# A four-layer forward and backward pass on one core: gradient operands stored by column group, the last attention products on the common ring, dz products three tiles late

## The chip, the cores and the metric

The kernel runs on one core of one Trainium2 chip. A core has TensorE (PE in the profile: matmuls and transposes; PEld is its weight loads), VectorE (DVE), ScalarE (ACT), GpSimd (POOL) and SyncE (SP), and 16 DMA engines that all DMA queues share. Matmul results land in PSUM and are copied out by VectorE or ScalarE; everything else lives in SBUF (128 partitions) or in DRAM. The metric is the device time of one execution in microseconds (us), as a median over runs.

## The reference

Four residual layers on x [2048, 512], A, B, A, B, sharing weights between the two A and between the two B, and then the gradients of x and of all five weight matrices for a given grad_out, in bf16:

```python
def _A_ref(x, wqkv, wo):                       # linear attention, 32 heads of 16
    q, k, v = heads(x @ wqkv)
    phi = lambda t: jnp.where(t > 0, t + 1, jnp.exp(t)) + 1e-6
    pq, pk = phi(q), phi(k)
    kv = jnp.einsum("bhsd,bhse->bhde", pk, v)
    z = jnp.einsum("bhsd->bhd", pk)
    num = jnp.einsum("bhqd,bhde->bhqe", pq, kv)
    den = jnp.einsum("bhqd,bhd->bhq", pq, z)[..., None] + 1e-6
    return merge_heads(num / den) @ wo
def _B_ref(x, w_gate, w_up, w_down):           # F = 1376
    return (_sigmoid(x @ w_gate) * (x @ w_up)) @ w_down
x = x + _A_ref(_layernorm(x), A_wqkv, A_wo)
x = x + _B_ref(_layernorm(x), B_w_gate, B_w_up, B_w_down)
x = x + _A_ref(_layernorm(x), A_wqkv, A_wo)
x = x + _B_ref(_layernorm(x), B_w_gate, B_w_up, B_w_down)
out = x;  gradients = vjp of this with grad_out
```

A weight gradient is a product over all 2048 rows: for instance the gradient of w_up is (normalised x)^T times the gradient of the product x @ w_up, [512, 2048] x [2048, 1376], summed over both B layers.

## The kernel before, in words

The 2048 rows are 16 tiles of 128 (NST = 16); 512 columns are four chunks of 128 (NDC), 1376 columns eleven, the last of 96 (NFC). Layers are numbered 0 (A), 1 (B), 2 (A), 3 (B).

**Forward.** Per A layer kq_fwd and then ab_fwd, which interleaves the attention output of one tile with the gated layer of the next. ab_fwd keeps what the backward pass needs in DRAM: h (the normalised input), ssd, and the gated product hh (stored at L705 into part 0 of `hdd`, a DRAM tile [2048, 3, 1376], L108).

**Backward, pass 1** goes through the row tiles and carries the gradient of x. b_bwd_p1 (gated layers) loads ssd per tile, makes dd (gradients of the up and gate products, two halves of 1376) and stores it at L839 into parts 1 and 2 of `hdd`. a_bwd_p1 (attention) has two loops. The first, per tile: a POOL cast of the gradient (L994), transposes through PSUM (L287), the products dp (L1002), an ACT copy of dp (L1005), on VectorE a product (L1007) and a sum per head, cneg (L1009), a POOL copy of cneg to bf16 (L1012), four small matmuls dz (L988) that add up in one PSUM tile, a POOL product t_t (L1017), and three VectorE operations (L1020, L1024, L1025) that make dq, stored two tiles at a time (L1028) into the left half of `dqk`, [2048, 1024] (L101). The dz matmuls of a tile are written down after the next tile's dp. Then G = g^T pqn, 64 matmuls (L1035), with the last tile's dz ahead of its second quarter. The second loop makes dk, stores it into the right half of `dqk` (L1133) and loads dq again (dq_ld, L1090).

**Backward, pass 2** makes the weight gradients. The columns are cut into groups of 256 (the last one 96); a "set" is a tile [128, 16, 256] that holds one such group for all rows, loaded by p2_set (L879–882) out of the row-major DRAM tile, so 2048 pieces of 512 B. p2_cols_group (L889–912) multiplies it with h_all: 64 matmuls of 128x256 (L903); the first layer of a pair leaves its result as a partial in DRAM, the second (final) loads that partial into dw_stg (L894), adds it on VectorE (L908) and writes the output (L912). b_bwd_p2 (L915–942) does w_down (L933, evacuation in dw_evac, L858–869), w_up and w_gate; a_bwd_p2 (L945–951) the q and k columns of wqkv, in four sets. Their resources R are a ring of three set buffers, two staging buffers and two PSUM buffers, all loads on SP's DMA queue.

**The last part.** The order of the calls is written out (L223–237): b_bwd_p1(3), a_bwd_p1(2), b_bwd_p2(3), b_bwd_p1(1), a_bwd_p2(2), a_bwd_p1(0), b_bwd_p2(1), a_small_grads, a_bwd_p2(0). The last two use resources RT of their own: pool t_big, three more set buffers (t_sets), four PSUM buffers (t_psum), and loads on ACT's DMA queue (L875, L881, L894). a_small_grads (L1168–1190) makes the gradient of wo and of the v columns of wqkv: 8 and 32 small matmuls, eight ACT copies into two fin_o buffers, eight outputs of 128 KB.

The code is written in a tile framework: its scheduler fixes one static order for each engine from the order of the calls, priorities and its own cost model, and uses pass 2's matmuls to fill gaps of pass 1. Semaphores between engines and DMAs follow from the tiles. On one queue, instructions issue in order, each waiting for its own inputs and free buffers.

Of the kernel before, what the change touches and what calls it, by code (L numbers as in the profile page):

```python
# [16 lines left out]
S = 2048  # L17
# [11 lines left out]
EPS = 1e-6  # L29
NB = 4  # L30


# [18 lines left out]
def kernel(  # L51
# [42 lines left out]
    for l in range(4):  # L94
        d = {}
        d["h"] = dram.tile([S, D], BF16, name=f"sv_h{l}")
        d["gbf"] = dram.tile([S, D], BF16, name=f"sv_gbf{l}")
        if l % 2 == 0:
            for nm in ("hT", "pqn", "phq", "pk"):
                d[nm] = dram.tile([S, D], BF16, name=f"sv_{nm}{l}")  # L100
            d["dqk"] = dram.tile([S, 2 * D], BF16, name=f"sv_dqk{l}")  # L101
            d["X"] = dram.tile([D, D], BF16, name=f"sv_X{l}")
            for nm, w in SMALL:
                d[nm] = dram.tile([D, w], BF16, name=f"sv_{nm}{l}")
            d["MT"] = dram.tile([D, D], BF16, name=f"sv_MT{l}")
        else:
            d["ssd"] = dram.tile([S, 2, F], BF16, name=f"sv_ssd{l}")
            d["hdd"] = dram.tile([S, 3, F], BF16, name=f"sv_hdd{l}")  # L108
        k.sv[l] = d
# [75 lines left out]
    if True:  # L185
# [26 lines left out]
        def mk_out1_cb(o1stg):  # L212
            o1cur = {}

            def out1_cb(st):
# [3 lines left out]
                if st % 2 == 1:  # L219
# [9 lines left out]
        b_bwd_p2(k, R, 1, True, list(range(NFC)))  # L229
        RT = P2Res(k,  # L230
                   big=bctx.enter_context(tc.tile_pool(name="t_big", bufs=1)),
                   sets=bctx.enter_context(tc.tile_pool(name="t_sets", bufs=3)),
                   stage=R.stage,
                   psum=bctx.enter_context(tc.tile_pool(name="t_psum", bufs=4, space=PSUM)),
                   set_w=2 * P, dma=[nc.scalar], pfx="ta")
        a_small_grads(k, RT.big, R.stage, RT.psum)
        a_bwd_p2(k, RT, 0, True)


# [339 lines left out]
def ab_fwd(k, A, ln, nxt=None, out_cb=None, extra=(), x_src=None):  # L579
# [3 lines left out]
    with ExitStack() as ctx:  # L583
# [85 lines left out]
        for st in range(NST):  # L669
# [34 lines left out]
            nc.sync.dma_start(out=sv["ssd"][rows(st), :, :], in_=ssd_t[:])  # L704
            nc.sync.dma_start(out=sv["hdd"][rows(st), 0, :], in_=hh_t[:])  # L705
            prev = T
# [64 lines left out]
def b_bwd_p1(k, l):  # L771
# [4 lines left out]
    with ExitStack() as ctx:  # L776
# [41 lines left out]
        for st in range(NST):  # L818
            g_bf, gT = gp.prep(st)
            ssd = ld.tile([P, 2, F], BF16, name="ssd_ld")  # L820
            nc.sync.dma_start(out=ssd[:], in_=sv["ssd"][rows(st), :, :])
            T = dict(st=st, h=hld.get(st), g=g_bf,
                     dd=wide.tile([P, 2, F], BF16, name="dd_t"),
                     ddT=wide.tile([P, 2, NFC, P], BF16, name="ddT"))
            dd = T["dd"]
            for fs in range(3):
                c0, w = FSL[fs]
                dhh_ps = ps_dhh.tile([P, 512], F32, name="dhh_ps")
                for jc in range(NDC):
                    nc.tensor.matmul(dhh_ps[:, 0:w], lhsT=gT[:, jc, :], rhs=k.wdT[:, jc, c0:c0 + w],  # L830
                                     start=(jc == 0), stop=(jc == NDC - 1))
                nc.vector.tensor_tensor(dd[:, 0, c0:c0 + w], dhh_ps[:, 0:w], ssd[:, 0, c0:c0 + w], ALU.mult)  # L832
                nc.vector.tensor_tensor(dd[:, 1, c0:c0 + w], dhh_ps[:, 0:w], ssd[:, 1, c0:c0 + w], ALU.mult)  # L833
                if fs >= 1:
                    transposes(T, fs - 1)
            if prev is not None:
                finish(prev)
            transposes(T, 2)
            nc.sync.dma_start(out=sv["hdd"][rows(st), 1:3, :], in_=dd[:])  # L839
            prev = T  # L840
# [3 lines left out]
class P2Res:  # L844

    def __init__(self, k, big, sets, stage, psum, set_w=P, dma=None, pfx="p2"):
        self.k, self.big, self.sets, self.stage, self.psum, self.set_w = k, big, sets, stage, psum, set_w
        self.pfx = pfx
        self.dma = dma or [k.nc.sync]
        self.i = 0  # L850
# [20 lines left out]

def p2_load_all(k, R, src, name):
    t = R.big.tile([P, NST, D], BF16, name=name)
    for b in range(NST // NB):
# [3 lines left out]

def p2_set(k, R, src2d, c0, w):  # L879
    t = R.sets.tile([P, NST, R.set_w], BF16, name="p2_set")  # L880
    R.eng().dma_start(out=t[:, :, 0:w], in_=src2d[:, c0:c0 + w].rearrange("(n p) f -> p n f", p=P))  # L881
    return t


# [30 lines left out]
def b_bwd_p2(k, R, l, final, fcs, h_all=None, g_all=None):  # L915
# [6 lines left out]
    for g0 in range(0, len(fcs), nper):  # L922
# [3 lines left out]
        w = sum(widths)  # L926
        st_t = p2_set(k, R, sv["hdd"][:, 0, :], c0, w)
        for j, fc in enumerate(grp):
# [10 lines left out]
        for i, nm in ((1, "wu"), (2, "wg")):  # L939
            st_t = p2_set(k, R, sv["hdd"][:, i, :], c0, w)  # L940
            p2_cols_group(k, R, h_all, st_t, w, k.dwp[nm], k.outs[nm], c0, final)
# [3 lines left out]
def a_bwd_p2(k, R, l, final):  # L945
    sv = k.sv[l]
    h_all = p2_load_all(k, R, sv["h"], R.pfx + "_a1")
    nper = R.set_w // P
    for j0 in range(0, 2 * NDC, nper):
        st_t = p2_set(k, R, sv["dqk"], j0 * P, nper * P)  # L950
        p2_cols_group(k, R, h_all, st_t, nper * P, k.dwp["wqkv"], k.outs["wqkv"], j0 * P, final)


def a_bwd_p1(k, R, l, mk_out_cb=None):
# [6 lines left out]
    with ExitStack() as ctx:  # L961
# [8 lines left out]
        with tc.tile_pool(name=f"ab_all{l}", bufs=1) as allp, \  # L970
# [21 lines left out]
            for st in range(NST):  # L992
# [8 lines left out]
                for jc in range(NDC):  # L1001
                    nc.tensor.matmul(dp_ps[:], lhsT=gT[:, jc, :], rhs=k.MT[:, jc, :],  # L1002
                                     start=(jc == 0), stop=(jc == NDC - 1))
                dp = work.tile([P, D], BF16, name="dp")
                nc.scalar.copy(dp[:], dp_ps[:])  # L1005
# [4 lines left out]
                                        negate=True)  # L1010
                cneg_bf = small.tile([P, H], BF16, name="cneg_bf")
                nc.gpsimd.tensor_copy(cneg_bf[:], cneg[:])  # L1012
                if dzq:
                    accum_dz(*dzq.pop())
                dzq.append((st, cneg_bf))
                t_t = work.tile([P, D], BF16, name="t_t")
                nc.gpsimd.tensor_tensor(t_t[:].rearrange("p (h e) -> p h e", h=H),  # L1017
# [8 lines left out]
                if st % NB2 == NB2 - 1:  # L1026
                    b = st // NB2
                    nc.sync.dma_start(out=sv["dqk"][batch_rows(b, NB2), 0:D].rearrange("(n p) d -> p n d", p=P),  # L1028
                                      in_=phld.cur[:])
            for jc in range(NDC):  # L1030
                if jc == 1:
                    accum_dz(*dzq.pop())
                ps = ps_mm.tile([P, D], F32, name="dp_ps")
# [49 lines left out]
        with tc.tile_pool(name=f"ab_stg2{l}", bufs=2) as stg, \  # L1083
# [5 lines left out]
            pkld = BatchLoader(k, stg, sv["pk"], "pk_ld", nb=NB2)  # L1089
            dqld = BatchLoader(k, stg, sv["dqk"], "dq_ld", nb=NB2)  # L1090
            hTld = BatchLoader(k, stg, sv["hT"], "hT_ld", nb=NB2)
# [16 lines left out]
            for st in range(NST):  # L1108
                pk_st = pkld.get(st)
                dq_st = dqld.get(st)  # L1110
                hT_st = hTld.get(st)
# [19 lines left out]
                if st % NB2 == NB2 - 1:  # L1131
                    b = st // NB2
                    nc.sync.dma_start(  # L1133
                        out=sv["dqk"][batch_rows(b, NB2), D:2 * D].rearrange("(n p) d -> p n d", p=P),
                        in_=dkst[:])
                if prev is not None:
# [9 lines left out]


SMALL = (("G", D), ("XT", D), ("kvbd", P), ("dkvbd", P))

# [71 lines left out]
```

## Time and profile before

| what | value |
|---|---|
| median of 3 runs | 1381.03 us (1379.69 to 1385.11) |
| the profiled execution's own time | 1379.42 us |
| its span in the profile | 1377.7 us |
| TensorE busy | 1234.0 us, 90% |
| mean granted TensorE clock | 0.972 |
| packets under 512 B, under 2 KB, in all | 28688, 240528, 259066 |
| DMA queue q1 (SP): MB, share of 16 engines | 247.30, 56.0% |
| DMA queue q10 (ACT): MB, share of 16 engines | 7.34, 1.9% |
| sv_hdd<-dd_t, 32 stores of 688 KB, issue to landing | 3.7 us |
| sv_hdd<-hh_t, 32 stores of 344 KB | 2.3 us |
| p_set<-sv_hdd, 30 wide sets of 1024 KB | 7.5 us |

The stages on the profile's time axis (us): forward up to 510; b_bwd_p1(3) 520 to 674; a_bwd_p1(2) first loop to 738, second loop to 825; b_bwd_p2(3) to 905; b_bwd_p1(1) to 1055; a_bwd_p1(0) first loop 1086 to 1144, second loop 1150 to 1228; b_bwd_p2(1) to 1337; a_small_grads to 1344; the last q and k sets to 1373.7; end 1377.7.

How to read it: an engine's busy time counts only its instructions' own time. A timeline line has start, duration, engine, line, operation, output and inputs, shape and count; in brackets is the idle time before it and what ended that. A windows line has, for each engine, busy time and number of instructions, then the granted TensorE clock as a share of full speed, the mean busy share of the 16 DMA engines (it can pass 1.00, since packets overlap) and the rate.

### The profile page before, as it was taken

Reading aid. Unit: us, or ns where it says so; the run is one execution under the profiler, and the core shown is the slowest. Engines: PE = TensorE matmul, PEld = TensorE weight load, DVE = VectorE, ACT = ScalarE, POOL = GpSimd, SP = SyncE. Lnnn points to the kernel's source line nnn. Section 1 sums busy time; section 2 is a strip of 40 time slices with the busy share of each in tenths; the row PEclk is TensorE's granted clock in tenths of the full one; section 3 lists DMA queues with packets and bytes.
Section 4 is the critical chain, followed back from the end, with each engine's and each line's share of the span. In section 5 each row is a group of like instructions: output and inputs, shape, how many; then the busy total and the mean of one; then the engine's idle time right before and its main releaser. Section 6 shows DMA issues by size and latency. Waiting matters only on the chain. (4 is left out here: it accounts for less than half of the span.)

```text
span 1377.7 us, 22244 instructions
## 1 busy us (share of the span) xinstructions
PE 1234.0 (90%) x8628; PEld 719.4 (52%) x8628; DVE 700.1 (51%) x1344; ACT 568.6 (41%) x1060; POOL 313.9 (23%) x534
## 2 busy tenths in 40 slices
PE   5958888896899978999889999999999989996998
PEld 2424444442455544555455557765555645564777
DVE  5577545456865435556485650035564385641211
ACT  6435666662566753444333441134443323520000
POOL 5046444402644430000351000001101440110000
PEclk9979999998899998999999999999999999998999
DMA  9413433332334459654765649796555946559963
GB/s 317 163 56 138 153 133 145 139 138 92 116 151 174 186 199 323 223 188 163 220 184 170 193 138 323 170 274 228 188 184 189 291 131 203 183 148 312 253 161 94
DMA packets 259066, 256.06 MB, mean 186 GB/s; under 512 B 28688, under 2 KB 240528, under 8 KB 258960
## 3 DMA queue, kind: packets, MB, share of 16 engines
q1 hardware_dynamic: 246480, 247.30, 56.0%
q10 hardware_dynamic: 12480, 7.34, 1.9%
q8 instruction: 67, 1.10, 0.3%
q14 instruction: 39, 0.32, 0.1%
HBM read 135.69 MB, written 118.92 MB: 185 GB/s over the span
## 5 line engine op out<-in xcount | busy, mean ns | idle before, releaser
L903 PE MATMUL p_ps<-p_set,p_a 128*128 128x256 bf16 (+1 forms) x1792 | 193.7, 266 | 11.1 <-DVE dw_stg L908 7.9
L903 PEld LDWEIGHTS <-p_a 128*128 128x128 bf16 x1792 | 160.9, 99 | 33.4 <-issue 8.1
L799 ACT COPY ddT<-T_ps 128x1024 bf16<-128x1024 bf16 (+1 forms) x96 | 83.0, 868 | 105.0 <-PE T_ps L797 104.9
L692 POOL TENSOR_TENSOR ssd_t<-hh_t,oms 128x512 bf16<-128x512 bf16 (+1 forms) x96 | 102.6, 1070 | 100.3 <-ACT oms L690 47.6
L720 DVE SCALAR_TENSOR_TENSOR junk<-t_sb,h_ld 128x512 bf16<-128x512 f32 x64 | 45.8, 716 | 142.6 <-ACT t_sb L718 142.6
L811 PEld LDWEIGHTS <-ddT 128*128 128x128 bf16 (+1 forms) x704 | 66.0, 97 | 69.3 <-issue 10.5
L718 ACT ACTIVATE t_sb<-dh_ps,rstd_all 128x512 f32<-128x512 f32 x64 | 44.0, 687 | 134.9 <-issue 60.8
L811 PE MATMUL dh_ps<-wuT,ddT 128*128 128x512 bf16 (+1 forms) x352 | 95.7, 379 | 4.2 <-ACT t_sb L718 0.9
L722 POOL TENSOR_SCALAR ab<-c 128x2 f32<-128x2 f32 x64 | 12.3, 193 | 373.9 <-DVE junk L720 373.9
L683 PE MATMUL g_ps<-wg,hT 128*128 128x512 bf16 (+1 forms) x384 | 96.6, 366 | 0.0
L686 PE MATMUL u_ps<-wu,hT 128*128 128x512 bf16 (+1 forms) x384 | 94.6, 363 | 0.0
L832 DVE TENSOR_TENSOR dd_t<-dhh_ps,ssd_ld 128x512 bf16<-128x512 f32 (+1 forms) x96 | 60.5, 630 | 57.2 <-issue 49.8
L830 PE MATMUL dhh_ps<-wdT,gT 128*128 128x512 bf16 (+1 forms) x384 | 87.0, 362 | 2.5 <-ACT gT L296 2.5
L691 DVE TENSOR_TENSOR hh_t<-u_ps,ssd_t 128x512 bf16<-128x512 f32 (+1 forms) x96 | 60.7, 633 | 55.9 <-PE u_ps L686 29.5
L933 PE MATMUL p_ps<-p_a,p_set 128*128 128x512 bf16 (+1 forms) x352 | 83.6, 379 | 1.4 <-DMA p_set<-sv_hdd 1.4
L652 PE MATMUL y_ps<-wd,hhT 128*128 128x512 bf16 (+1 forms) x352 | 81.6, 380 | 0.2 <-DVE x L654 0.2
L811 PE MATMUL dh_ps<-wgT,ddT 128*128 128x512 bf16 (+1 forms) x352 | 81.3, 379 | 0.0
L797 PEld LDWEIGHTS <-dd_t 128*128 128x128 bf16 (+1 forms) x704 | 50.2, 100 | 40.7 <-DVE dd_t L832 18.6
L797 PE MATMUL T_ps<-ident,dd_t 128*128 128x128 bf16 (+1 forms) x704 | 66.0, 219 | 3.6 <-DVE dd_t L832 3.3
L908 DVE TENSOR_TENSOR dw_stg<-p_ps,dw_stg 128x512 bf16<-128x512 f32 (+1 forms) x32 | 20.6, 648 | 87.8 <-PE p_ps L903 64.5
L688 ACT ACTIVATE ssd_t<-g_ps 128x512 bf16<-128x512 f32 (+1 forms) x96 | 53.1, 553 | 27.3 <-PE g_ps L683 26.8
L833 DVE TENSOR_TENSOR dd_t<-dhh_ps,ssd_ld 128x512 bf16<-128x512 f32 (+1 forms) x96 | 60.1, 626 | 0.0
(203 smaller groups left out, 2226.6 us busy)
## 6 DMA issues: line engine op xcount, KB each, us to landing
p_set<-sv_hdd SPq DMA_DIRECT2D x30, 1024.0 KB, 7.5
sv_ssd<-ssd_t SPq DMA_DIRECT2D x32, 688.0 KB, 3.1
ssd_ld<-sv_ssd SPq DMA_DIRECT2D x32, 688.0 KB, 5.4
sv_hdd<-dd_t SPq DMA_DIRECT2D x32, 688.0 KB, 3.7
sv_hdd<-hh_t SPq DMA_DIRECT2D x32, 344.0 KB, 2.3
h_ld<-sv_h SPq DMA_DIRECT2D x32, 256.0 KB, 3.6
p_a<-sv_h SPq DMA_DIRECT2D x12, 512.0 KB, 6.3
sv_h<-h_all SPq DMA_DIRECT2D x8, 512.0 KB, 3.3
```

What stands on the lines that cost most here:

```text
L652: nc.tensor.matmul(y_ps[:], lhsT=T["hhT"][0:r, fc, :], rhs=k.wd[0:r, fc, :], start=(fc == 0), stop=(fc == NFC - 1))
L683: nc.tensor.matmul(g_ps[:, 0:w], lhsT=hT[:, kc, :], rhs=k.wg[:, kc, c0:c0 + w], start=(kc == 0), stop=(kc == NDC - 1))
L686: nc.tensor.matmul(u_ps[:, 0:w], lhsT=hT[:, kc, :], rhs=k.wu[:, kc, c0:c0 + w], start=(kc == 0), stop=(kc == NDC - 1))
L691: nc.vector.tensor_tensor(hh_t[:, c0:c0 + w], u_ps[:, 0:w], ssd_t[:, 0, c0:c0 + w], ALU.mult)
L692: nc.gpsimd.tensor_tensor(ssd_t[:, 1, c0:c0 + w], hh_t[:, c0:c0 + w], oms[:, 0:w], ALU.mult)
L797: nc.tensor.transpose(tps[0:r, a, i, :], dd[:, a, fc * P:fc * P + r], k.ident[:])
L799: nc.scalar.copy(ddT[:, :, fcs[0]:fcs[0] + nfull, :], tps[:, :, 0:nfull, :])
L811: nc.tensor.matmul(dh_ps[:], lhsT=T["ddT"][0:r, a, fc, :], rhs=wT[0:r, fc, :], start=(i == 0), stop=(i == n_mm - 1))
L830: nc.tensor.matmul(dhh_ps[:, 0:w], lhsT=gT[:, jc, :], rhs=k.wdT[:, jc, c0:c0 + w], start=(jc == 0), stop=(jc == NDC - 1))
L832: nc.vector.tensor_tensor(dd[:, 0, c0:c0 + w], dhh_ps[:, 0:w], ssd[:, 0, c0:c0 + w], ALU.mult)
L903: nc.tensor.matmul(psv[:, icl, :], lhsT=lhs_all[:, st, ic * P:(ic + 1) * P], rhs=set_t[:, st, 0:W], start=(st == 0), stop=(st == NST - 1))
L933: nc.tensor.matmul(ps[0:r, :], lhsT=st_t[:, st, j * P:j * P + r], rhs=g_all[:, st, :], start=(st == 0), stop=(st == NST - 1))
```

## The change

Three things change.

1. `hdd` becomes [3, 5, 128, 16, 256] (part, column group, partition, tile, column) with the last 96 columns in a DRAM tile of their own, `hdl` [3, 128, 16, 96]; `dqk` becomes [4, 128, 16, 256]. A wide set is one contiguous megabyte, 8 KB for each partition. The store of hh becomes two DMAs, that of dd three, each store of dq and dk two, and each load of dq two: 144 DMAs more in all. In SBUF nothing changes its place.
2. The resources RT go. The last attention sets use R like all others (three ring buffers, two PSUM buffers, SP's queue), with h_all in a pool of its own; a_small_grads is called after them, on R's PSUM buffers.
3. In a_bwd_p1's first loop dp has three buffers, the bf16 copy of cneg is on ACT with five buffers, and the dz matmuls of a tile are written down three tiles later (DZLAG = 3), what is left of them ahead of the second quarter of G.

```diff
+GW = 256
+NG = F // GW
...
-            d["dqk"] = dram.tile([S, 2 * D], BF16, name=f"sv_dqk{l}")
+            d["dqk"] = dram.tile([2 * D // GW, P, NST, GW], BF16, name=f"sv_dqk{l}")
-            d["hdd"] = dram.tile([S, 3, F], BF16, name=f"sv_hdd{l}")
+            d["hdd"] = dram.tile([3, NG, P, NST, GW], BF16, name=f"sv_hdd{l}")
+            d["hdl"] = dram.tile([3, P, NST, F - NG * GW], BF16, name=f"sv_hdl{l}")
...
-        RT = P2Res(k,
-                   big=bctx.enter_context(tc.tile_pool(name="t_big", bufs=1)),
-                   sets=bctx.enter_context(tc.tile_pool(name="t_sets", bufs=3)),
-                   stage=R.stage,
-                   psum=bctx.enter_context(tc.tile_pool(name="t_psum", bufs=4, space=PSUM)),
-                   set_w=2 * P, dma=[nc.scalar], pfx="ta")
-        a_small_grads(k, RT.big, R.stage, RT.psum)
-        a_bwd_p2(k, RT, 0, True)
+        tail = bctx.enter_context(tc.tile_pool(name="t_big", bufs=1))
+        R.big_h = tail
+        a_bwd_p2(k, R, 0, True)
+        a_small_grads(k, tail, R.stage, R.psum)
...
-            nc.sync.dma_start(out=sv["hdd"][rows(st), 0, :], in_=hh_t[:])
+            nc.sync.dma_start(out=sv["hdd"][0, :, :, st, :].rearrange("g p w -> p g w"),
+                              in_=hh_t[:, 0:NG * GW].rearrange("p (g w) -> p g w", g=NG))
+            nc.sync.dma_start(out=sv["hdl"][0, :, st, :], in_=hh_t[:, NG * GW:F])
...
-            nc.sync.dma_start(out=sv["hdd"][rows(st), 1:3, :], in_=dd[:])
+            for a in range(2):
+                nc.sync.dma_start(out=sv["hdd"][1 + a, :, :, st, :].rearrange("g p w -> p g w"),
+                                  in_=dd[:, a, 0:NG * GW].rearrange("p (g w) -> p g w", g=NG))
+            nc.sync.dma_start(out=sv["hdl"][1:3, :, st, :].rearrange("a p w -> p a w"), in_=dd[:, :, NG * GW:F])
...
+        self.big_h = None
...
-def p2_load_all(k, R, src, name):
-    t = R.big.tile([P, NST, D], BF16, name=name)
+def p2_load_all(k, R, src, name, pool=None):
+    t = (pool or R.big).tile([P, NST, D], BF16, name=name)
-def p2_set(k, R, src2d, c0, w):
+def p2_set(k, R, src):
-    R.eng().dma_start(out=t[:, :, 0:w], in_=src2d[:, c0:c0 + w].rearrange("(n p) f -> p n f", p=P))
+    R.eng().dma_start(out=t[:, :, 0:src.shape[-1]], in_=src)
+
+
+def hdd_group(sv, i, g):
+    return sv["hdd"][i, g, :, :, :] if g < NG else sv["hdl"][i, :, :, :]
...
-        st_t = p2_set(k, R, sv["hdd"][:, 0, :], c0, w)
+        st_t = p2_set(k, R, hdd_group(sv, 0, c0 // GW))
...
-            st_t = p2_set(k, R, sv["hdd"][:, i, :], c0, w)
+            st_t = p2_set(k, R, hdd_group(sv, i, c0 // GW))
-    h_all = p2_load_all(k, R, sv["h"], R.pfx + "_a1")
+    h_all = p2_load_all(k, R, sv["h"], R.pfx + "_a1" if R.big_h is None else "t_a1", R.big_h)
-        st_t = p2_set(k, R, sv["dqk"], j0 * P, nper * P)
+        st_t = p2_set(k, R, sv["dqk"][j0 * P // GW, :, :, :])
+
+
+def dqk_store(k, sv, half, b, nb, src):
+    n = D // GW
+    for g in range(n):
+        k.nc.sync.dma_start(out=sv["dqk"][half * n + g, :, b * nb:(b + 1) * nb, :],
+                            in_=src[:, :, g * GW:(g + 1) * GW])
...
-                dp = work.tile([P, D], BF16, name="dp")
+                dp = work.tile([P, D], BF16, name="dp", bufs=3)
-                cneg_bf = small.tile([P, H], BF16, name="cneg_bf")
-                nc.gpsimd.tensor_copy(cneg_bf[:], cneg[:])
-                if dzq:
-                    accum_dz(*dzq.pop())
+                cneg_bf = small.tile([P, H], BF16, name="cneg_bf", bufs=DZLAG + 2)
+                nc.scalar.copy(cneg_bf[:], cneg[:])
+                if len(dzq) > DZLAG:
+                    accum_dz(*dzq.pop(0))
...
-                    nc.sync.dma_start(out=sv["dqk"][batch_rows(b, NB2), 0:D].rearrange("(n p) d -> p n d", p=P),
-                                      in_=phld.cur[:])
+                    dqk_store(k, sv, 0, b, NB2, phld.cur[:])
-                if jc == 1:
-                    accum_dz(*dzq.pop())
+                while jc == 1 and dzq:
+                    accum_dz(*dzq.pop(0))
...
-            dqld = BatchLoader(k, stg, sv["dqk"], "dq_ld", nb=NB2)
...
-                dq_st = dqld.get(st)
+                if st % NB2 == 0:
+                    dq_cur = stg.tile([P, NB2, D], BF16, name="dq_ld")
+                    for g in range(D // GW):
+                        nc.sync.dma_start(out=dq_cur[:, :, g * GW:(g + 1) * GW],
+                                          in_=sv["dqk"][g, :, st:st + NB2, :])
+                dq_st = dq_cur[:, st % NB2, :]
...
-                    nc.sync.dma_start(
-                        out=sv["dqk"][batch_rows(b, NB2), D:2 * D].rearrange("(n p) d -> p n d", p=P),
-                        in_=dkst[:])
+                    dqk_store(k, sv, 1, b, NB2, dkst[:])
...
+DZLAG = 3
```

## The prediction, made before the changed kernel ran

> **What bounds the kernel now.** I read the page's busy shares first, then its 40 slices, then the windows of the stretches that the change touches, then the timeline there.
>
> The page's parts 1 and 2:
>
> ```profile
> PE 1234.0 (90%) x8628; PEld 719.4 (52%) x8628; DVE 700.1 (51%) x1344; ACT 568.6 (41%) x1060; POOL 313.9 (23%) x534
> ...
> PE   5958888896899978999889999999999989996998
> ...
> DMA  9413433332334459654765649796555946559963
> ```
>
> TensorE is the bound: 90% of 1377.7 us. A change can only give back its idle time or its slow-clock time. The thin place late in the run is slice 37 (1240 to 1274 us): PE 6, DMA 9. Windows of 25 us there, then the other stretches that the change touches (columns: engine busy time, granted clock, DMA share):
>
> ```profile
> core 0: us, PE busy (x) PEld busy (x) DVE busy (x) ACT busy (x) POOL busy (x), PEclk, DMA share, GB/s
> 1225.00:1250.00 25.00, 18.23 (x135) 12.83 (x134) 5.40 (x9) 0.59 (x1) 0.62 (x1) 0.90 1.02 285
> 1250.00:1275.00 25.00, 20.31 (x130) 13.66 (x129) 2.77 (x4) 0.00 (x0) 0.00 (x0) 0.90 1.17 301
> ...
> 1300.00:1325.00 25.00, 25.00 (x201) 19.35 (x199) 4.98 (x8) 0.00 (x0) 0.00 (x0) 1.00 0.80 187
> ...
> 575.00:660.00 85.00, 83.65 (x565) 43.89 (x564) 51.50 (x95) 36.15 (x63) 1.74 (x9) 1.00 0.48 163
> 674.00:738.00 64.00, 52.39 (x377) 30.45 (x377) 44.11 (x85) 21.36 (x38) 34.28 (x49) 0.95 0.59 171
> 1086.00:1144.00 58.00, 48.84 (x335) 25.21 (x335) 43.21 (x88) 18.31 (x34) 23.00 (x32) 1.00 0.52 159
> ```
>
> From 1225 to 1275 us all DMA engines are full and TensorE idles 11.5 of 50 us at a clock of 0.90; once the rush is over (1300) it is full at clock 1.00. In the steady b_bwd_p1 loop (575) the DMA is half free. In the two attention loops (674, 1086) TensorE is 82 to 84% busy. The timeline names the rush. DMAs of the ACT queue and a sum on VectorE:
>
> ```profile
> 1230.18 0.39 ACTq L881 DMA_DIRECT2D p_set<-sv_dqk  x1
> 1231.08 9.92 ACTq L875 DMA_DIRECT2D ta_a<-sv_h  x4
> 1248.56 1.29 DVE L908 TENSOR_TENSOR dw_stg<-p_ps,dw_stg 128x512 bf16<-128x512 f32 x2 [12.27 <-DMA dw_stg<-dwp_wu]
> ```
>
> and TensorE, with idle time before each group in brackets:
>
> ```profile
> 1249.30 9.92 PE L903 MATMUL p_ps<-p_set,p_a 128*128 128x256 bf16 x64 [6.75 <-DVE dw_stg L908]
> 1260.64 7.08 PE L933 MATMUL p_ps<-p_a,p_set 128*128 128x512 bf16 x32 [1.42 <-DMA p_set<-sv_hdd]
> 1270.07 3.65 PE L903 MATMUL p_ps<-p_set,p_a 128*128 128x256 bf16 x32 [2.35 <-DVE dw_stg L868]
> 1274.64 3.65 PE L903 MATMUL p_ps<-p_set,p_a 128*128 128x256 bf16 x32 [0.91 <-DVE dw_stg L868]
> 1279.41 7.15 PE L903 MATMUL p_ps<-p_set,p_a 128*128 128x256 bf16 x64 [1.12 <-DVE dw_stg L908]
> 1337.05 1.89 PE L1178 MATMUL p_ps<-G_ld,kvbd_ld 128*128 128x512 bf16 x8
> 1341.66 1.10 PE L1186 MATMUL p_ps<-dkvbd_ld,XT_ld 128*128 128x128 bf16 x16 [1.80 <-ACT fin_o L1180]
> 1344.10 29.59 PE L903 MATMUL p_ps<-p_set,ta_a 128*128 128x256 bf16 x256 [1.33 <-ACT fin_o L1189]
> ```
>
> The ACT queue brings ta_a and three sets (5 MB) needed only from 1344 on, right beside the sets and the 256 KB dw_stg partials that SP brings for now. VectorE waits 12.27 us for one partial, so no PSUM buffer comes free and TensorE waits 6.75 us.
>
> **The last product stretch (ring).** From 1228.65 (first L933 group) to 1373.70 (last L903) lie 145.05 us. Full rate, by undisturbed groups: a column group is 6.91 (L933, 32 matmuls) + 13.97 (L903, 128), four of them 83.52; the last narrow one 3.45 + 5.45 = 8.90; the four q/k sets are 2 x 13.97 = 27.94. Sum 120.36, surplus 24.69. It is made of the five bracketed stalls in 1249–1279, 6.75 + 1.42 + 2.35 + 0.91 + 1.12 = 12.55; of the slot of the small gradients, 1337.05 to 1344.10 = 7.05; of slow clock, 9.92 − 7.15 = 2.77 and 29.59 − 27.94 = 1.65; 0.67 is in small gaps. In the changed program these 5 MB stand in SP's queue behind the sets that come before them, three ring buffers ahead at most, so the rush has no cause. SP is also the queue of the ta_a, G, XT, kvbd and dkvbd loads now, and these stand between the set loads; and with two PSUM buffers instead of four the last sets have the spacing of all earlier ones (7 us per 64 matmuls against 0.65 us of evacuation each half), which at 1300–1325 gave no idle time. What can be late next is the first q set: it reuses a buffer of the narrow wd5/wu5/wg5 sets, and a lone 1 MB load takes 6.1 us, while the two narrow sets left then cover 5.45: 0.65 late. ta_a's 2 MB (5 us at 400 GB/s) may still run beside it. I put 1.5 us on both (0 to 4). −24.7 + 1.5 = **−23.2**.
>
> **The end.** Now 4.00 us lie between the last matmul (1373.70) and the end. The small gradients come last in the changed program: 8 + 32 matmuls, eight ACT copies, eight 128 KB outputs through two fin_o buffers. Their pace is a row of this trace: first copy 1338.13, last copy ends 1348.16, 10.03 us, each pair waiting for an earlier output. 0.5 us from the last L903 to the first result (half of 1337.05–1338.13) + 10.0 + 1.8 for the last output's landing + 1.0 to the end = 13.3, so **+9.3**. It has no cover: nothing follows. Bounds: +7 (outputs faster, since the DMA is otherwise empty) and +11.
>
> **The attention loops (dz).** The changed program's order on each engine is known: the first dz group stands at the same place on TensorE, since the scheduler already kept two to three tiles between a dz and its tile. So its 2.69 us stall (the wait is for pqn_all's load, 8.5 us on VectorE) stays. What changes: after the last dz 40 matmuls of G (L1035) are left instead of 48 in the first loop, 35 instead of 40 in the second; these no longer stand behind the late tail: 8 x 0.216 = 1.7 and 5 x 0.216 = 1.1. The cneg_bf copy leaves POOL, where it took 0.27 us (median) and up to 0.67 ahead of t_t; the ACT copy of that size starts earlier: −0.5 each loop. VectorE waits for t_t on POOL 4.2 and 5.1 us in the two loops, of which I take 1.5 off each (0 to all). In the second loop 26 fewer filler matmuls (L903, L912) stand before G's end, they run later at 0.109 each: +2.8. Loop 1: −1.7 − 0.5 − 1.5 = −3.7; loop 2: −1.1 − 0.5 − 1.5 + 2.8 = −0.3. **−4.0.** What is queued behind the new wait: ACT now waits for cneg (VectorE's L1009) ahead of the next gT and dp copies, which TensorE's next tile needs; ACT is 33% busy there, and the third dp buffer lets ACT empty dp_ps one tile further ahead of VectorE. If that wait bites in a third of 32 tiles with the 0.6 us of a copy, it is +6, so the loops lie between −9 and +2.
>
> **The layout.** Sets: 2048 pieces of 512 B become 128 stretches of 8 KB. A lone set load took 6.1 us (172 GB/s for 1 MB, issue to landing); stretches with pieces over 1 KB ran at 350 to 410 GB/s against 285 to 301 in the rush. I give each of the 38 wide sets 0.5 us less of DMA time, worth nothing to TensorE where it does not wait. Stores pay: dd (704 KB) was two long pieces per row, about 1.75 us of all engines at 400 GB/s; now it is 1280 pieces of 512 B and 256 of 192 B. At the 285–295 GB/s of the 512 B output rows it is 2.4, and 0.5 for the narrow part: 2.9, **+1.2 a step**; hh +0.55. Cover: a b_bwd_p1 step lasts 9.25 us with the DMA busy 0.52 of it (4.8), so 4.4 us are free; ab_fwd has 0.35 of 10.7 us. TensorE pays nothing in the steady steps. In the first 55 us of the first backward loop the share is 0.86 already, five steps x 1.2 = 6 us at the most; I take **+1** (0 to 6). SP issues 144 more DMAs at 0.36–0.5 us, some 60 us of an engine whose instructions nobody waits for except the ssd_ld behind the dd store (0.8 us later, two tiles ahead of use).
>
> The Trainium skill, page "DMA: Bandwidth & Descriptors", section "Rules for kernel authors", speaks against splitting stores: it asks for few large transfers, and says that one under 64 KB is mostly overhead. By its 2 us of fixed cost a DMA (section "Anatomy of one DMA", stated there for the GpSimd path), my estimate is that 144 more would cost 288 us if they stood on the path; the trace has no instruction of TensorE waiting for a store of sv_hdd, so I keep zero. Section "Latency and other measured facts" of the same page says that row pitches at large powers of two (512 KiB and up) lose DMA rate; the new pitch of a partition is 8 KB, which it does not list and no run here shows yet.
>
> **Sum.** −24.7 + 1.5 + 9.3 − 4.0 + 1.0 = −16.9 on the profiled execution's 1379.42 us (span 1377.7): 1362.5. The median of the three runs is 1381.03, 1.6 higher, so I say **1364**. The best ends of all terms (−24.7, 0, +7, −9, 0 = −26.7) give 1354, the worst (−24.7, +4, +11, +2, +6 = −1.7) 1379.
>
> **Rivals.**
> *The change of dz does not do what it says.* For it: the built order keeps the first dz at the same place. Then the loops give 0 (and the second costs its 2.8): 1368 to 1371, inside the main case.
> *The rush is not only the ACT queue's.* SP now has the same 5 MB in its own queue within the same 145 us; against it, at 1300–1325 a share of 0.80 left TensorE full. If 10 of the 12.55 us of stalls come back, or move to the q sets at 1330: 1374, and 1378 with the slow clock's 4.4 too. It is a ring of three whose next load waits for a matmul to release it.
> *Slower: small pieces at a pitch of 8 KB.* All 128 partitions of a store write 512 B (and 192 B) at the same offset of successive 8 KB blocks; the rows of before (5.5 KB, contiguous) do not show that. It decides from the point at which the dd store's 1.75 us grows past the free time, 1.75 + 4.4 = 6.2 us, below 114 GB/s. At 100 GB/s it takes 7.05, a step lasts 4.8 − 1.75 + 7.05 = 10.1 instead of 9.25, and 32 steps cost 0.87 x 32 = +28: 1392 as a median, and 1410 at 92 GB/s. Against it: outputs of 512 B at a pitch of 3 KB run at 285 or more.
>
> **How the numbers follow.** Main case 1358–1371: 0.58. Both loops at their better ends and no tail stalls, 1350–1358: 0.08. The rush stays in part, 1371–1380: 0.16. About as before, 1380–1388 (stalls and end at their worst together): 0.05. Small pieces, 1388–1410: 0.13. The range 1354 to 1380 leaves out about half of the 0.08, the 0.05 and the 0.13: a little over 0.2. Half a per cent, 6.9 us, is about what a measurement can tell: faster means below 1374.1, slower above 1387.9. Faster: 0.58 + 0.08 + 0.06 of the rush case = 0.72; within: 0.10 + 0.05 = 0.15; slower 0.13.
>
> **What would show it.** Right: no L875 or L881 on the ACT queue; TensorE idle under 4 us between the last attention part and the last L903, clock near 1.00; eight fin_o copies about 10 us long at the very end; b_bwd_p1 steps of 9.25 us with DMA share near 0.65. Wrong: TensorE or VectorE waiting for ssd_ld, h_ld or sets inside b_bwd_p1, a dd store that lands after more than 7 us, waits for p_set<-sv_dqk at the first q set, ACT idle on cneg with TensorE idle on gT.

## The result, and the profile after

The changed kernel takes 1361.98 us (median of 4 runs, 1359.01 to 1365.61) against 1381.01; the ratio is 0.9858 (1.4% less), 95% interval 0.9826 to 0.9891. A second set gave 1362.19 and a ratio of 0.9874 (0.9845 to 0.9902). The forecast was 1364. The profiled execution took 1363.26 us with a span of 1361.4.

Parts 1 and 2 of the page after:

```profile
PE 1225.3 (90%) x8628; PEld 717.1 (53%) x8628; DVE 706.3 (52%) x1344; ACT 573.9 (42%) x1092; POOL 304.4 (22%) x502
...
PE   5957888896799997999979999999999979999987
...
DMA  9413443432244559766654739678665855659873
...
DMA packets 266235, 256.08 MB, mean 188 GB/s; under 512 B 43280, under 2 KB 251024, under 8 KB 261264
```

The dent of PE 6 late in the run is gone; what is thin now is the last slice but one and the last. Windows of the kernel after (columns as in those of before):

```profile
1220.00:1245.00 25.00, 25.00 (x197) 19.07 (x195) 5.37 (x8) 0.00 (x0) 0.00 (x0) 1.00 1.01 324
1245.00:1270.00 25.00, 25.00 (x181) 17.51 (x180) 5.00 (x8) 0.00 (x0) 0.00 (x0) 1.00 1.01 328
1270.00:1295.00 25.00, 25.00 (x190) 18.40 (x188) 4.84 (x7) 0.00 (x0) 0.00 (x0) 1.00 0.73 235
1295.00:1320.00 25.00, 21.53 (x258) 18.51 (x257) 4.79 (x9) 0.00 (x0) 0.00 (x0) 0.98 0.79 186
...
575.00:660.00 85.00, 83.67 (x569) 44.19 (x568) 51.49 (x95) 36.75 (x64) 1.73 (x9) 1.00 0.56 163
674.00:738.00 64.00, 52.07 (x409) 31.39 (x410) 47.70 (x89) 24.20 (x54) 28.44 (x32) 1.00 0.50 160
```

The DMA engines are as full as before (1.01), at a higher rate, but TensorE no longer waits and keeps its clock. One stall is left, at the first q set, and then there is the end:

```profile
1312.82 0.82 DVE L917 TENSOR_TENSOR dw_stg<-p_ps,dw_stg 128x192 bf16<-128x192 f32 x2 [1.57 <-DMA dw_stg<-dwp_wu]
1313.67 0.38 SPq L921 DMA_DIRECT2D out_dram<-dw_stg  x1
1314.14 0.46 SPq L903 DMA_DIRECT2D dw_stg<-dwp_wg  x1
...
1319.17 0.62 DVE L917 TENSOR_TENSOR dw_stg<-p_ps,dw_stg 128x192 bf16<-128x192 f32 x2 [5.53 <-DMA dw_stg<-dwp_wg]
1319.58 29.58 PE L912 MATMUL p_ps<-p_set,t_a 128*128 128x256 bf16 x256 [3.47 <-DVE dw_stg L917]
...
1352.73 1.07 ACT L1198 CAST fin_o<-p_ps 128x512 bf16<-128x512 f32 x2 [1.58 <-DMA out_dram<-fin_o]
...
1355.17 1.07 ACT L1207 CAST fin_o<-p_ps 128x512 bf16<-128x512 f32 x2 [1.37 <-DMA out_dram<-fin_o]
...
1357.59 1.07 ACT L1207 CAST fin_o<-p_ps 128x512 bf16<-128x512 f32 x2 [1.35 <-DMA out_dram<-fin_o]
```

The stall is hardly the q set's: TensorE's last narrow product ends at 1316.10, and the set's first load, issued at 1310.56, lands at 1316.55. VectorE waits 5.53 us for the last narrow partial (dwp_wg), whose load was issued only at 1314.14, right behind an output that waits for VectorE.

Where the time went, by landmarks on TensorE in the two profiles (us). Lines named in the text are those of the kernel before; a fence has those of its own kernel. "First loop" and "second loop" are, as in the prediction, the dp and dz loops of a_bwd_p1(2) and of a_bwd_p1(0), each from its first transpose to the first product with Mv in the loop that follows; "filler" are products of pass 2 that the scheduler puts behind the last of pass 1. Up to the first dhh product (L830, the start of the backward pass) 521.2 to 520.5 (−0.7); first loop 76.0 to 73.4 (−2.5); second loop 71.7 to 67.1 (−4.6); filler 6.6 to 9.75 (+3.2); last stretch, first L933 to last L903, 145.2 to 125.8 (−19.4); end 4.0 to 12.25 (+8.2); the rest −0.5. Sum −16.3, as the spans say. Of the −19.4, 7.05 is the slot of the small gradients, which the change only moves: it comes back in the +8.2.

### The profile page after: what moved, and what is told of

It reads as the page before. It is cut to its first block, busy times and chain, and to the rows that moved or that the text cites. A ratio compares the mean times of both kernels' runs of the same rounds, so it can differ in the third digit from the quotient of the medians.

```text
span 1361.4 us, 22444 instructions
## 1 busy us (share of the span) xinstructions
PE 1225.3 (90%) x8628; PEld 717.1 (53%) x8628; DVE 706.3 (52%) x1344; ACT 573.9 (42%) x1092; POOL 304.4 (22%) x502
## 5 line engine op out<-in xcount | busy, mean ns | idle before, releaser
L912 PE MATMUL p_ps<-p_set,p_a 128*128 128x256 bf16 (+1 forms) x1792 | 189.0, 263 | 0.0
L798 PEld LDWEIGHTS <-dd_t 128*128 128x128 bf16 (+1 forms) x704 | 50.3, 100 | 40.3 <-DVE dd_t L833 18.3
```

The source lines that it names most:

```text
L798: nc.tensor.transpose(tps[0:r, a, i, :], dd[:, a, fc * P:fc * P + r], k.ident[:])
L912: nc.tensor.matmul(psv[:, icl, :], lhsT=lhs_all[:, st, ic * P:(ic + 1) * P], rhs=set_t[:, st, 0:W], start=(st == 0), stop=(st == NST - 1))
```

## The experiments

Profiles of kernels with the same forward code differ by up to 5.7 us before the first dhh product (517.3 to 522.9), so stages are compared from there on. The medians and ratios are from repeated runs against before on the same chip; the pair in brackets is the ratio's 95% interval. Different sets ran on different chips.

**e1, layout alone.** The changed kernel with parts 2 and 3 undone.

```diff
-        tail = bctx.enter_context(tc.tile_pool(name="t_big", bufs=1))
...
+        a_small_grads(k, RT.big, R.stage, RT.psum)
+        a_bwd_p2(k, RT, 0, True)
...
-                nc.scalar.copy(cneg_bf[:], cneg[:])
+                nc.gpsimd.tensor_copy(cneg_bf[:], cneg[:])
```

> Only part 1 of the change: the DRAM layout of hdd and dqk with its split stores; the last sets stay on ACT's queue, dz as before. Theory (the layout is about neutral, the last ring is what pays): 1379 to 1383 us; in the last product stretch TensorE still idles 8 us or more ahead of L903/L933 groups, and the last stretch from the first L933 to the last L903 keeps 140 to 146 us. Rival (cheaper sets are what ended the rush): 1366 to 1372, that stretch 130 us or less.

1375.47 us against 1379.06, ratio 0.9969 (0.9952 to 0.9986). The last stretch is 141.1 us, so 4.1 less. Both theories miss the time: the layout is not neutral, and it does not end the rush (the stretch stays in the theory's 140 to 146). TensorE's stalls and VectorE's wait before the longest, from the timeline of e1:

```profile
1245.00 7.15 PE L916 MATMUL p_ps<-p_set,p_a 128*128 128x256 bf16 x64 [1.85 <-DVE dw_stg L921]
...
1263.40 0.69 DVE L877 TENSOR_TENSOR dw_stg<-p_ps,dw_stg 128x512 bf16<-128x512 f32 x1 [10.52 <-DMA dw_stg<-dwp_wd]
1264.14 6.32 PE L916 MATMUL p_ps<-p_set,p_a 128*128 128x256 bf16 x32 [5.09 <-DVE dw_stg L877]
1271.23 10.64 PE L916 MATMUL p_ps<-p_set,p_a 128*128 128x256 bf16 x96 [0.77 <-DVE dw_stg L877]
```

7.7 us of stalls instead of 12.6: again waits for partials, shorter in sum. From 1250 to 1275 us the DMA moves 365 GB/s instead of 301; that this is why the waits are shorter is likely, not shown.

**e2, ring alone.** The kernel before with part 2 only.

```diff
-        a_small_grads(k, RT.big, R.stage, RT.psum)
-        a_bwd_p2(k, RT, 0, True)
+        R.big_h = tail
+        a_bwd_p2(k, R, 0, True)
+        a_small_grads(k, tail, R.stage, R.psum)
```

> Only part 2: last attention sets through the common ring on SP's queue, small gradients last; row-major layout and dz as before. Theory: the last stretch falls from 145 to about 126 us and the end grows by 8.2 us, so 11 us less: 1370 (1367 to 1373). Rival (cheaper sets are what ended the rush): the sets of 512 B pieces still come late, 10 us of stalls stay, and with the longer end it is 1380 to 1388.

1374.03 us, ratio 0.9968 (0.9950 to 0.9986). The last stretch is 130.5 us, 14.7 less, the end 12.2. It is the theory's side, a little above its 1367 to 1373, and its stretch is 4.7 us longer than the changed kernel's. No set comes late; two partials do, one of w_down in the middle and the narrow one at the q set. From e2's timeline:

```profile
1283.95 0.69 DVE L865 TENSOR_TENSOR dw_stg<-p_ps,dw_stg 128x512 bf16<-128x512 f32 x1 [8.12 <-DMA dw_stg<-dwp_wd]
...
1284.69 11.99 PE L900 MATMUL p_ps<-p_set,p_a 128*128 128x256 bf16 x96 [2.65 <-DVE dw_stg L865]
...
1329.65 30.84 PE L900 MATMUL p_ps<-p_set,t_a 128*128 128x256 bf16 x256 [3.19 <-DVE dw_stg L905]
```

**e3, dz alone.** The kernel before with part 3 only.

```diff
+                cneg_bf = small.tile([P, H], BF16, name="cneg_bf", bufs=DZLAG + 2)
+                nc.scalar.copy(cneg_bf[:], cneg[:])
+                if len(dzq) > DZLAG:
+                    accum_dz(*dzq.pop(0))
```

> Only part 3: dz products three tiles late, cneg copy on ACT, three dp buffers. Theory (what the two traces show between the landmarks of the two loops): first loop 2.5 us shorter, second loop 4.6 us shorter with 3.2 us of filler products given back later: 1377 (1375 to 1379). Rival 1 (the scheduler had the distance already, so it does nothing): 1380 to 1382. Rival 2 (the loops gained from the layout or from chance): loops within 0.5 us of before.

1381.29 us, ratio 1.0021 (1.0005 to 1.0037): a small loss, so rival 1 by its time, though the loops did move. First loop 76.8 instead of 76.0, second 67.7 instead of 71.7 with 3.6 us of filler given back, last stretch 2.3 us longer.

**e4, ACT's queue to SP's.** The kernel before, one argument dropped.

```diff
-                   set_w=2 * P, dma=[nc.scalar], pfx="ta")
+                   set_w=2 * P, pfx="ta")
```

> The kernel before with one word changed: the last attention sets, ta_a and their partials go through SP's queue instead of ACT's; they keep their own three set buffers and four PSUM buffers, and the small gradients stay ahead of them. If the order in one queue is what ends the rush: the stalls of 12.6 us ahead of L903/L933 groups fall under 5, the small gradients' slot of 7 us and the end of 4 us stay: 1371 (1368 to 1374). If the buffers are what holds the loads back, they still rush in ahead of need: 1377 to 1383.

1371.35 us, ratio 0.9946 (0.9929 to 0.9963). With buffers of its own and nothing else changed, the last stretch falls to 134.6 us, and the stalls to 5.1, just above the "under 5" expected. So the order in one queue does it. It does not end the stalls: in e4's timeline most of them stand at the end of the rush and not at its start, one for a set and two for partials:

```profile
1298.42 3.67 PE L903 MATMUL p_ps<-p_set,p_a 128*128 128x256 bf16 x32 [1.18 <-DMA p_set<-sv_hdd]
1303.90 3.65 PE L903 MATMUL p_ps<-p_set,p_a 128*128 128x256 bf16 x32 [1.81 <-DVE dw_stg L868]
1308.84 7.15 PE L903 MATMUL p_ps<-p_set,p_a 128*128 128x256 bf16 x64 [1.29 <-DVE dw_stg L908]
```

One dropped argument gives more than all of part 2: by the profiles the stretch is 10.6 us shorter and the end stays at 4.0, where e2 has −14.7 and +8.2. The small gradients, moved to the very end, cost 8.2 us there, where their slot cost 7.05. By the medians e4 is 2.7 us below e2, though the intervals overlap.

**e5 to e7: what dz adds.** e5 is the changed kernel again, e6 the changed kernel with part 3 undone, e7 the changed kernel with one line of it undone:

```diff
-                nc.scalar.copy(cneg_bf[:], cneg[:])
+                nc.gpsimd.tensor_copy(cneg_bf[:], cneg[:])
```

> The changed kernel itself, beside the kernel before and the three kernels of this set. The three parts alone gave ratios of 0.997, 0.997 and 1.002, which add up to 0.996, while the whole gave 0.986. If the whole is more than its parts: 0.986 again, about 1360. If the first figure was chance: 0.993 to 0.996, 1369 to 1374.

> Parts 1 and 2 together (layout and ring), dz as before. If dz brings what the whole has over its parts (the loops of the changed kernel were 2.5 and 4.6 us shorter, 3.2 us of filler given back): 1364 to 1368, 4 us above the changed kernel. If dz brings nothing, as alone: 1358 to 1362, within 2 us of the changed kernel. If layout and ring do not add up: above 1369.

> The changed kernel with the copy of cneg to bf16 back on POOL; five buffers, three tiles late, three dp buffers stay. If the copy on ACT holds up ACT's next dp copy (TensorE waited 5.9 us for dp copies in the first loop, 1.7 before): first loop 1 to 4 us shorter, 1358 to 1361. If ACT helps, as the prediction has it (0.5 a loop and 1.5 of VectorE's waits): 3 to 4 us longer, 1363 to 1366.

Against 1380.04: e5 1362.19 (0.9874), e6 1367.32 (0.9914; 0.9889 to 0.9938), e7 1362.98 (0.9885; 0.9860 to 0.9910). On top of layout and ring, part 3 is worth 5 us by the medians, and from the first dhh product on 4.6 us by the profiles (840.7 against 845.3). Neither case of e7 came true: with the copy on ACT (e5) or on POOL (e7) the medians are 0.8 us apart and the first loop takes 73.2 and 73.1 us. The waits on TensorE from 674 to 738 us show why, in the changed kernel's second profile (e5) and in e7 (us in total, times, longest):

```profile
PE dz_ps L1004 <- ACT cneg_bf L1028: 5.9, 6, 2.1
PE dp_ps L1018 <- ACT dp L1021: 5.1, 5, 1.8
```

```profile
PE dz_ps L1004 <- POOL cneg_bf L1028: 9.1, 8, 2.5
PE dp_ps L1018 <- ACT dp L1021: 1.7, 3, 1.0
```

What dz no longer waits for, dp waits for: ACT stands at cneg ahead of the next dp copy.

**e8 to e10: the end repaired.** e9 has eight fin_o buffers and a third staging buffer for partials; e8 has these and the small gradients ahead of the q and k sets, on four PSUM buffers of their own; e10 is e8 with dz as before.

```diff
-        o = stg.tile([P, D], BF16, name="fin_o")
+        o = pool.tile([P, D], BF16, name="fin_o", bufs=8)
...
-    return R.stage.tile([P, NDC * R.set_w], BF16, name="dw_stg", tag=f"dw_{tag}")
+    return R.stage.tile([P, NDC * R.set_w], BF16, name="dw_stg", tag=f"dw_{tag}",
+                        bufs=3 if tag == "a" else 2)
...
-        a_bwd_p2(k, R, 0, True)
-        a_small_grads(k, tail, R.stage, R.psum)
+        tps = bctx.enter_context(tc.tile_pool(name="t_psum", bufs=4, space=PSUM))
+        a_small_grads(k, tail, R.stage, tps)
+        a_bwd_p2(k, R, 0, True)
```

> The changed kernel with the end repaired: small gradients ahead of the q and k sets on four PSUM buffers of their own, eight fin_o buffers, and three staging buffers for partials. If the end of 12.2 us is the eight copies' pace through two buffers, and the 3.5 us stall at the first q set is the partial's staging buffer: end back to 4.0, small gradients about 4 us in the middle instead of 7, stall under 1: 9 to 11 us less than the changed kernel, 1350 to 1352. If the stall is the set load itself: 3 us less gained, 1353 to 1356.

> The changed kernel with the small gradients still last, but eight fin_o buffers instead of two and three staging buffers for partials instead of two. If the two fin_o buffers set the pace at the end (the last three pairs of copies each waited 1.4 to 1.6 us for an output to land): the end falls from 12.2 to 7.5 to 8.5 us. If the stall of 2.8 to 3.5 us at the first q set is the partial's staging buffer: it falls under 1 and the 256 products of the q and k sets take 28.1 us instead of 29.6. Both: 1355 to 1357. Rival for the stall (the narrow partial's own load time and its place in SP's queue behind an output): stall stays at 2 to 3.5 us, 1358 to 1360.

> The repaired version (e8) with dz as before. A second pair for dz: if dz is worth about 4.7 us in this surrounding, 1359 to 1361 against the 1355 of e8 (ratio to before 0.987 to 0.988). If the 5 us between e6 and the changed kernel were chance: 1354 to 1356.

e8 1355.34 us (0.9839; 0.9812 to 0.9867), e9 1353.24 (0.9806; 0.9782 to 0.9830), e10 1359.74 (0.9841; 0.9817 to 0.9866, in e9's set). In e9 the end falls from 12.2 to 8.5 us and the stall to 0.95; in e8 the end is 4.0 and the small gradients take 3.35 us in the middle. From the first dhh product on the two profiles are alike (834.2 us each), against 840.7 in e5, and the medians are 7 and 9 us below e5's; by the ratios it is 5 and 9, and e8's interval overlaps e5's. e8's forecast of 1350 to 1352 was too low, e9's of 1355 to 1357 a little high. e9's two edits were not tried apart, but they act at different places. In e9 the load of the narrow partial stands ahead of the q set's and of the output, 1.2 us before the narrow products begin on TensorE; in the changed kernel it stands 3.8 us after that. First e9, then the same place in e8:

```profile
1310.42 0.50 SPq L904 DMA_DIRECT2D dw_stg<-dwp_wg  x1
1311.86 0.34 SPq L886 DMA_DIRECT2D p_set<-sv_dqk  x1
...
1318.21 28.11 PE L913 MATMUL p_ps<-p_set,t_a 128*128 128x256 bf16 x256 [0.95 <-DVE dw_stg L918]
```

```profile
1315.81 1.89 PE L1198 MATMUL p_ps<-G_ld,kvbd_ld 128*128 128x512 bf16 x8
...
1317.53 1.95 PE L1206 MATMUL p_ps<-dkvbd_ld,XT_ld 128*128 128x128 bf16 x32
...
1319.32 28.11 PE L914 MATMUL p_ps<-p_set,t_a 128*128 128x256 bf16 x256
```

The 256 products take 28.11 us after no stall or one of 0.95, and 29.58 after one of 3.47. e10, without dz, is 6.5 us above e9 by the medians of one set. By the profiles from the first dhh product on it is 1.3 us above e8 (835.5 against 834.2): loops and filler are 3.9 us shorter with dz (152.8 against 156.7), but two stages that dz doesn't touch are 2.4 us longer. By the ratios, from two chips, e8 and e10 are the same (0.9839 and 0.9841), where e10 was forecast at 0.987 to 0.988. So on the repaired kernel dz's loops are shorter, and what that is worth in time stays open, between nothing and 6 us.

**e11 and e12: what dz needs.** e11 is part 2 with part 3, e12 part 1 with part 3; the edits are those above.

> Parts 2 and 3 without the layout. dz alone gave 1.002, dz on top of layout and ring 0.996. If the rush on ACT's queue is what took dz's gain (its last stretch was 2.5 us longer, 147.5 us instead of 145.0), the ring alone lets it show: 0.992 to 0.994 (the ring alone gave 0.997), 1369 to 1371. If dz needs the layout: 0.997 or more, 1375 or more, with the first loop no shorter than before's 76.0 us.

> Parts 1 and 3 without the ring. If dz's gain is lost to the rush on ACT's queue, it stays lost: 0.996 to 0.999 (layout alone gave 0.997), 1375 to 1379, first loop 73 to 74 us as in the changed kernel but the last stretch longer than the 141.1 us of the layout alone. If the layout is what dz needs: 0.992 to 0.994, 1369 to 1371.

e11 1374.99 us (0.9953; 0.9936 to 0.9970), e12 1370.56 (0.9926; 0.9909 to 0.9943). So the ratios of all combinations, each with an interval of about 0.002 to 0.003 to either side:

| | dz as before | dz changed |
|---|---|---|
| row-major, ACT's queue | 1 | 1.0021 (e3) |
| row-major, ring | 0.9968 (e2) | 0.9953 (e11) |
| layout, ACT's queue | 0.9969 (e1) | 0.9926 (e12) |
| layout, ring | 0.9914 (e6) | 0.9874 (e5) |

e11 lies between its two forecasts, so the ratios alone would not separate layout from ring; the profiles do. Both loops and the filler together change with dz by +0.5 us in e3 and +0.4 in e11 (against e2), but by −5.3 in e12 (against e1) and −5.4 in e5 (against e6). Part of this is ground that the layout itself loses: without dz the same stages are 2.0 us longer in e1 than in the kernel before and 1.7 longer in e6 than in e2. So it is the layout that dz needs, not the ring; my theory of the rush fell. The first loop's G (first L1035 to its last) shows one place: 18.3 us in e3 and e11, 15.6 in e12 and in the changed kernel. The timeline of VectorE and TensorE ahead of the last dz, first e3, then e12:

```profile
720.92 0.42 DVE L1024 TENSOR_TENSOR t_t<-dp,t_t 128x512 bf16<-128x512 bf16 x1 [0.23 <-POOL t_t L1017]
721.26 1.28 DVE L1020 SCALAR_TENSOR_TENSOR phq_ld<-phq_ld,rden_all 128x512 bf16<-128x512 bf16 x2
722.47 0.75 DVE L1025 TENSOR_TENSOR phq_ld<-t_t,phq_ld 128x512 bf16<-128x512 bf16 x2
723.13 1.28 DVE L1007 TENSOR_TENSOR prod<-dp,pqn_all 128x512 bf16<-128x512 bf16 x1
...
725.64 0.24 PE L988 MATMUL dz_ps<-cneg_bf,pqn_all 128*128 128x8 bf16 x4 [2.18 <-ACT cneg_bf L1012]
```

```profile
721.49 0.43 DVE L1044 TENSOR_TENSOR t_t<-dp,t_t 128x512 bf16<-128x512 bf16 x1 [0.23 <-POOL t_t L1037]
721.83 0.42 DVE L1027 TENSOR_TENSOR prod<-dp,pqn_all 128x512 bf16<-128x512 bf16 x1
722.16 1.29 DVE L1040 SCALAR_TENSOR_TENSOR phq_ld<-phq_ld,rden_all 128x512 bf16<-128x512 bf16 x2
...
725.02 0.24 PE L1008 MATMUL dz_ps<-cneg_bf,pqn_all 128*128 128x8 bf16 x4 [1.21 <-ACT cneg_bf L1032]
```

With the layout the static order on VectorE has the last tile's product ahead of four operations on dq, without it behind them. The product then runs beside POOL's t_t (1.28 us instead of 0.42; POOL has it from 723.03 to 724.13), dz waits 2.18 us instead of 1.21, and the clock falls in the next 4 us of G (0.57 from 726 to 730 us in e3, 1.00 in e12). e3 and e12 differ in the layout alone, so it is the layout that moves the scheduler's order; through which of its costs was not tried.

## Why the prediction was right, point by point

**Right: the ring and its cause.** The 5 MB rush on ACT's queue was the largest term, and e4 shows the cause by itself: the order in one queue, since the buffers stayed. The term was −23.2, measured −19.4. The part that failed is "what can be late next is the first q set": the set landed 0.45 us after the last narrow product, close to the forecast 0.65, but the narrow partial was late (a stall of 3.47 us, and 1.5 us of slow clock behind it; 5.4 us of surplus in all). In e9 its load goes out before the narrow products begin, and the stall is 0.95. The prediction never asked where the partial's load stands in SP's queue behind an output.

**Right: the end.** +9.3 against +8.2. The pace of two buffers was the mechanism: e9 with eight takes 8.5 us instead of 12.2.

**Right sum, wrong reasons: the loops.** −4.0 against −3.9 (−2.5 − 4.6 + 3.2), which is luck: the first loop was put at −3.7 and gave −2.5, the second at −0.3 and gave −1.4 with its filler. The first dz group kept its place as said, but its stall of 2.69 us did not stay: it is 1.50 in the changed kernel and 2.06 in e5 (and 2.65 to 3.77 in e8, e9 and e12, so it varies). The copy that leaves POOL is worth nothing (e7), since the new wait on ACT, which the prediction put at +6 where it bites, came: TensorE's waits for dp copies in the first loop grew from 1.7 to 5.9 us. VectorE's waits for POOL did fall there (4.1 to 1.8 us), but its busy time rose by 3.6 (44.1 to 47.7). In the second loop 3.2 of the 4.6 us are 29 filler products that only run later (the forecast had 26). What is gained lies partly in G, shorter by 0.7 us in the first loop and 1.1 in the second (put at 1.7 and 1.1); the rest was not assigned. And it is gained only with the layout (e3, e11, e12), which no step of the prediction saw; the rival "does not do what it says" is right for dz alone.

**Mis-sized: the layout.** +1 against −0.3% alone (e1). The stores cost less than put: DMA share in the steady b_bwd_p1 loop 0.48 to 0.56, so 0.08 x 85 us over 9.2 steps = 0.74 us a step instead of 1.2, and the loop's length did not change (153.56 and 153.55 us). Cheaper sets were costed at nothing "where it does not wait", but in the rush TensorE did wait: in e1 the stalls fell by 4.8 us (sets landed in 5.6 us instead of 7.6, medians from 530 to 1230 us).

**The slower rival is out.** The wide dd stores, two of 320 KB each, land in 3.6 us after issue, as the one of 688 KB did (3.7). The rival of a rush that stays is partly true without the layout: e2 keeps stalls of 5.8 us.

**Size.** −16.9 on the profiled execution, measured 1379.42 to 1363.26 = −16.2. The misses of +3.8 (ring), −1.1 (end) and −2.2 (layout and the rest) nearly cancel, so it is partly luck that 1364 came 2 us from 1362.

The Trainium skill, page "DMA: Bandwidth & Descriptors", section "Rules for kernel authors", asks for few large transfers. The set loads do not test this: a set is one transfer of 1 MB in both kernels, and only its pieces grew, from 512 B to 8 KB (5.8 us to landing against 7.6). The split does: 144 more DMAs, 128 of them stores, cost nothing that a landmark shows, and no instruction of TensorE waits for such a store.

## What to carry to other kernels

Loads that are needed late belong in the queue behind those that are needed soon: a second queue that starts them early takes the rate from what TensorE is waiting for now, though all buffers are free. After such a repair, look at small things at the seam, a partial's staging buffer or two output buffers at the end; here they were worth a quarter to a half as much again. And where a scheduler sets the order, one part of a change is not worth the same alone: measure it in the place where it will stand.

## What the runs showed of the hardware

**The clock can fall after a short stall.** Windows behind the stall at the first q set, e5 (2.84 us of idle time) and then e9 (0.95 us), clock in the third column from the right:

```profile
1318.00:1322.00 4.00, 3.23 (x17) 2.36 (x17) 0.62 (x2) 0.00 (x0) 0.00 (x0) 0.64 1.00 318
1322.00:1326.00 4.00, 4.00 (x36) 3.48 (x34) 0.69 (x1) 0.00 (x0) 0.00 (x0) 0.93 0.65 257
1326.00:1330.00 4.00, 4.00 (x39) 3.58 (x37) 0.69 (x1) 0.00 (x0) 0.00 (x0) 1.00 0.33 82
```

```profile
1318.00:1322.00 4.00, 3.79 (x35) 3.40 (x35) 0.52 (x3) 0.00 (x0) 0.00 (x0) 1.00 0.93 273
```

A stall of 2.84 us costs 1.7 us more (29.78 against 28.11 for the same 256 products). In e3 the 2.18 us ahead of the last dz bring the clock to 0.57 for the next 4 us; the 1.21 us in e12 leave it at 1.00. But the length alone does not decide: in the same e3 a stall of 2.55 us leaves it at 1.00, and so do the 2.35 us at 1270.07 in the kernel before. From e3:

```profile
703.90 1.02 PE L1002 MATMUL dp_ps<-MT_X,gT 128*128 128x512 bf16 x3 [2.55 <-ACT dp L1005]
```

```profile
704.00:708.00 4.00, 3.16 (x19) 1.55 (x20) 3.86 (x8) 2.71 (x6) 2.00 (x2) 1.00 0.92 258
726.00:730.00 4.00, 3.78 (x11) 1.47 (x11) 3.65 (x13) 0.00 (x0) 0.86 (x1) 0.57 0.14 50
```

The page "TensorE: Matmul & The Clock Gate" of the Trainium skill, section "Part 1: The HAM clock gate", puts the fall after an idle window of about 3.4 us; the runs here show it after a stall of 2.2 us, and not after every longer one.

**VectorE beside POOL.** In the loops of the changed kernel VectorE's product of two bf16 tiles (prod) takes 0.42 us with POOL idle and 0.85 in the mean beside POOL's t_t product, up to 1.32. So work that is put closer together on the two engines can pay part of the wait that it saves.
